# The first Q, K and V of an attention kernel, loaded whole or by thirds

## The chip, the cores and the metric

The kernel runs on one core of a Trainium2 chip. A core has engines that run side by side, each with its own stream of instructions: TensorE (PE in the profile, with its weight loads as PEld), VectorE (DVE), ScalarE (ACT), GpSimd (POOL) and SyncE (SP). In this kernel SP issues every transfer between the chip's memory and the core's on-chip memory. 16 DMA engines carry them. PE writes its results into PSUM, here eight banks of 128 x 512 words; the others work on SBUF and PSUM. An engine that needs another's result waits on a semaphore.

The metric is the device time of one execution, in microseconds (us). Three runs of the kernel before gave 119.02, 119.18 and 119.19 us; the median is 119.18.

## The reference

A linear attention with cosine weights is followed by a mixture of low-rank adapters. Everything is float32; the inputs are eight batches of eight heads with 576 positions of 64 numbers.

```python
theta = np.pi / 2.0 * pos / S
def phi(x, c, s):
    r = np.maximum(x, 0.0)
    return np.concatenate([r * c, r * s], axis=-1)
q_p = phi(q, cos_w, sin_w)
k_p = phi(k, cos_w, sin_w)
kv = np.einsum('bhsf,bhsd->bhfd', k_p, v)   # per head: 128 x 64
z = np.sum(k_p, axis=2)
num = np.einsum('bhsf,bhfd->bhsd', q_p, kv)
den = np.einsum('bhsf,bhf->bhs', q_p, z)[..., None] + 1e-06
x = (num / den), heads side by side         # 4608 rows of 512
logits = x @ w_gate                         # 8 experts; the two largest count
w = softmax over the two
out = x + sum over the two: w_e * (x @ A[e]) @ B[e]
```

In the second half A[e] is 512 x 16 and B[e] is 16 x 512.

## The kernel before, in words

A batch's Q, K or V is one transfer of 1152 KB (batches 4 and 5, and 6 and 7, share one for Q and for K). In SBUF a position p of 0 to 63 holds nine neighbouring rows j = 0 to 8 of 64 numbers, for four heads, with the other four heads in partitions 64 to 127; so each partition gets four runs of 9 x 64 floats, 2304 bytes each, from memory.

The work is cut into named steps, and the text `ORDER` lists them in the order in which they are issued. Behind "=" stands the engine (S is ACT, V is DVE, G is POOL), behind "@" the buffer. Each engine does its own steps in the listed order; semaphores follow from the buffers. A program planned the text beforehand, with costs and times of its own, and the text is fixed in the file. The steps:

- `LQ0`, `LK0`, `LV0`, `LK1` ...: the loads, on SP (L388); `ldw` the three weight transfers (L356, L359, L361).
- `cK0.0` to `cK0.2` and `cQ0.0` to `cQ0.2`: cast a third of a batch (three of the nine j) to 16 bits, with the maximum with zero for K (L440, L442; Q at L302, L304, L306). `phiK0.j` and `phiQ0.j`: multiply the cast rows j by the tangent, which gives the second half of phi (L310, L313). `vs0.j`: V's row j times the cosine (L310, L313).
- `kv0.0` to `kv0.2`: 24 matmuls each for k_p^T v over three j, on PE (L500); they need the phiK and vs of these three j. `ke0` copies the result out of PSUM (L302, L306).
- `tq`: transposes Q for a tile of 128 rows on PE (L604); `eq` copies it out with the maximum with zero (L621, L623); `nd` multiplies it by kv (L647 with L662 where both halves are of one batch, L654 with L668 where they are of two); `rd` and `nx` divide (L687, L692); `tx` and `ex` transpose the result (L713, L302, L306); `za` multiplies by gate and A (L738); `mx`, `nt`, `ge`, `d`, `sg`, `w`, `zg` choose and weigh the experts (L749 to L783); `tz` and `ez` transpose that (L799); `dx` adds x and B's part (L837); `eo` copies out of PSUM (L302, L306); `st` stores three tiles or fewer (L855).
- `fill=n` puts n matmuls of no use on PE (L864), the first 41 of them while nothing has arrived.

A step of one load needs the whole transfer: `add_phi` gives every cast `[ld]` as what it waits for, and `vs` gives the loads of V. SP's transfers take turns on eight semaphores, so an issue also waits until the transfer eight issues before it has landed, where it has not been waited for already. There are 36 tiles; tiles 0 to 2 belong to batch 0, 3 to 5 to batch 1, 6 to 8 to both, and so on in pairs.

Of the kernel before, what the change touches and what calls it, by code (L numbers as in the profile page):

```python
# [86 lines left out]
phiQ3.0=S tx8@7 phiQ3.3=G tx9 eq10=S@1 zg5 phiQ3.4=G tq12@4 ex8=V@1 tz2@0 phiQ3.1=G za6@6 tz5@1
vs3.0=G@0 ez2=V@2 za7 za8 mx6@1 tq13 ez5=V@0 phiK3.1=G vs3.1=S phiQ3.5=V dx3@0 vs3.2=G
phiQ2.8=S eq12=V@0 dx4 vs3.4=G phiK3.0=S dx5@7 phiK3.2=G eo3=S@0 mx7 nd10@2 mx8 cQ3.2=G@2 eo5=V
nd11 phiQ3.2=S kv3.0@0 fill=2@7 rd10@0 vs3.3=G LQ6@0 nx10@3 vs3.7=S vs3.5=G phiQ3.8=S nt8=G  # L90
vs3.8=S phiK3.6=G ge8 tq14@2 phiK3.8=V phiK3.7=S phiQ3.6=G d8 tx10@4 phiQ3.7=V sg8 kv3.1
vs3.6=V cK4.0=S@0 w8=G tx11 cK4.1=V@4 LV6@0 za9@7 kv3.2 tq15 ex10=V@1 phiK4.3=G cK4.2=S@2 mx9@0
# [807 lines left out]
```

## Time and profile before

| | |
|---|---|
| median of three runs | 119.18 us |
| the profiled execution | 118.97 us |
| its span, first to last instruction | 117.2 us |
| mean granted TensorE clock | 0.985 of full |
| read and written | 28.85 MB and 9.44 MB |
| transfers on SP's queue | 15808 packets, 38.29 MB |

The profile is one execution. "Busy" is the time in which an engine worked; PE's is partly modelled, since matmuls overlap. A row of the timeline or of a group gives the line in the code, the engine, the operation, what it writes and reads with their shapes, and in brackets how long the engine stood idle before, with what ended the idle time. A row of the chain of waits is a stretch (start, duration) of the path that ended last, followed back from the end. Times in it count from the first instruction.

### The profile page before, as it was taken

The numbers are of one execution on the slowest core, as the hardware profiler recorded it, in microseconds if no ns is written. First come the engines' busy times: TensorE is split into PE (matmuls) and PEld (weight loads), VectorE is DVE, ScalarE is ACT, GpSimd is POOL, SyncE is SP. The second block draws the span as 40 slices with busy tenths as digits, with TensorE's granted clock in tenths as the row PEclk, the third lists the DMA queues.
The fourth block names the chain that finished last, engine by engine and source line by source line (L and its number), as shares of the span: only waits on it lengthen the run. The fifth ranks groups of instructions, "written<-read, shape, count | busy, mean of one in ns | idle before, by whom it ended". The sixth has DMA issues, their size and how long they took to land.

```text
span 117.2 us, 4510 instructions
## 1 busy us (share of the span) xinstructions
PE 97.0 (83%) x1930; PEld 72.4 (62%) x1939; DVE 86.0 (73%) x206; ACT 86.1 (73%) x132; POOL 62.2 (53%) x118
## 2 busy tenths in 40 slices
...
GB/s 42 401 399 391 390 392 392 392 304 395 392 389 391 391 391 391 385 393 389 388 393 385 392 385 391 388 417 424 363 56 6 233 299 19 168 369 163 336 394 187
DMA packets 15827, 38.57 MB, mean 329 GB/s; under 512 B 1728, under 2 KB 1728, under 8 KB 15808
## 3 DMA queue, kind: packets, MB, share of 16 engines
q1 hardware_dynamic: 15808, 38.29, 87.1%
...
q14 instruction: 4, 0.03, 0.1%
HBM read 28.85 MB, written 9.44 MB: 327 GB/s over the span
## 4 chain that ended last, share of the span: by engine, by line
PE 32%; DMA 27%; DVE 21%; issue 6%; POOL 6%; ACT 2%; SPq 2%; DVEq 0%; POOLq 0%
DMA v<-in_v_dram 27%; PE psum L837 8%; PE psum L604 7%; PE psum L738 5%; DVE qt L623 5%; PE psum L713 4%; DVE x L692 4%; PE psum L654 3%; POOL vb L313 2%; POOL qp L304 2%; SPq L388 2%; DVE xt L306 2%; DVE kp L313 1%; DVE rd L687 1%; POOL qp L313 1%
## 5 line engine op out<-in xcount | busy, mean ns | idle before, releaser
L604 PE MATMUL psum<-ident,qp 128*128 128x128 bf16 x288 | 21.4, 226 | 4.1 <-DVE qp L313 1.3
L692 DVE TENSOR_TENSOR x<-psum,rd 128x1024 bf16<-128x1024 f32 (+1 forms) x19 | 22.2, 1168 | 0.6
L604 PEld LDWEIGHTS <-qp 128*128 128x128 bf16 x288 | 18.0, 101 | 6.1 <-issue 2.3
L313 POOL TENSOR_SCALAR kp<-kp,tanw 128x256 bf16<-128x256 bf16 (+1 forms) x28 | 16.2, 590 | 5.7 <-ACT kp L440 3.1
L313 POOL TENSOR_SCALAR qp<-qp,tanw 128x256 bf16<-128x256 bf16 (+1 forms) x31 | 17.2, 569 | 3.7 <-ACT qp L302 3.4
L313 POOL TENSOR_SCALAR vb<-v,cosw 128x256 bf16<-128x256 f32 (+1 forms) x25 | 14.8, 604 | 7.7 <-DMA v<-in_v_dram 7.6
L440 ACT ACTIVATE kp<-k 128x768 bf16<-128x768 f32 (+1 forms) x12 | 12.4, 1055 | 5.8 <-DMA k<-in_k_dram 5.4
L623 DVE TENSOR_SCALAR qt<-psum 128x2048 bf16<-128x2048 bf16 x12 | 14.6, 1214 | 0.9 <-PE psum L604 0.8
L713 PE MATMUL psum<-ident,x 128*128 128x128 bf16 x144 | 12.1, 221 | 3.3 <-DVE x L692 3.2
L500 PE MATMUL psum<-vb,kp 64*128 64x65 bf16 x576 | 12.8, 190 | 2.2 <-issue 1.1
L304 POOL CAST qp<-q 128x768 bf16<-128x768 f32 (+1 forms) x9 | 9.8, 1107 | 9.0 <-DMA q<-in_q_dram 7.4
L864 PE MATMUL psum<-ident 128*128 128x512 bf16 (+1 forms) x53 | 13.3, 405 | 1.4 <-POOL ident masks.py:199 1.4
L837 PE MATMUL psum<-x,ident 128*64 128x512 bf16 (+1 forms) x47 | 13.4, 384 | 0.6 <-ACT zt L302 0.3
L738 PE MATMUL psum<-AW,xt 128*128 128x136 bf16 x144 | 13.0, 223 | 0.7 <-DVE m L749 0.5
L500 PEld LDWEIGHTS <-kp 64*128 64x128 bf16 x576 | 10.2, 94 | 4.4 <-issue 2.4
L713 PEld LDWEIGHTS <-x 128*128 128x128 bf16 x144 | 9.3, 114 | 4.6 <-DVE x L692 4.3
L621 ACT ACTIVATE qt<-psum 128x2048 bf16<-128x2048 bf16 (+1 forms) x7 | 11.3, 1628 | 0.4 <-PE psum L604 0.4
L654 PE MATMUL psum<-kv,qt 128*64 128x65 bf16 x384 | 9.8, 197 | 2.1 <-issue 1.2
L837 PE MATMUL psum<-Bb,zt 128*64 128x512 bf16 (+1 forms) x42 | 11.4, 379 | 0.1
L302 ACT COPY o<-psum 128x1024 f32<-128x1024 f32 (+1 forms) x11 | 8.7, 821 | 3.7 <-PE psum L837 3.5
L738 PEld LDWEIGHTS <-xt 128*128 128x128 bf16 x144 | 9.4, 98 | 3.2 <-issue 1.4
L302 ACT CAST qp<-q 128x768 bf16<-128x768 f32 (+1 forms) x8 | 7.9, 987 | 4.7 <-DMA q<-in_q_dram 4.7
...
## 6 DMA issues: line engine op xcount, KB each, us to landing
v<-in_v_dram SPq DMA_DIRECT2D x8, 1152.0 KB, 16.0
q<-in_q_dram SPq DMA_DIRECT2D x4, 1152.0 KB, 15.0
...
k<-in_k_dram SPq DMA_DIRECT2D x2, 2304.0 KB, 20.0
...
```

Source lines behind the costliest of these rows:

```text
L302: nc.scalar.copy(o_ap, i_ap)
L313: eng.tensor_scalar(out=o_ap, in0=i_ap, scalar1=by, scalar2=0.0, op0=ALU.mult, op1=ALU.add)
L440: nc.scalar.activation(o_ap, i_ap, AF.Relu)
L500: nc.tensor.matmul(out=psum[:, s + hp, h2 * W:(h2 + 1) * W], lhsT=kp[hp * 64:hp * 64 + 64, bi * H2 + h2, :], rhs=vb_t[hp * 64:hp * 64 + 64 ...
L604: nc.tensor.transpose(out=o_ap[:, h2, :, hi, :], in_=qv[:, bi * H2 + h2, :], identity=ident)
L623: nc.vector.tensor_scalar(out=o_ap, in0=i_ap, scalar1=0.0, scalar2=None, op0=ALU.max)
L654: nc.tensor.matmul(out=psum[hi * 64:hi * 64 + 64, s + g, x * W:(x + 1) * W], lhsT=qt[:, qi, h2, hp, hi, :], rhs=kv_t[KV[b]["kv"].slot][:, ...
L692: nc.vector.tensor_tensor(out=x_t[Y["x"].slot][:, 0:n].rearrange("p n (g i d) -> p (n g) i d", g=2, i=4), in0=f()[:, :, :, 0:D], in1=r().t ...
L713: nc.tensor.transpose(out=bank16(s, 1024)[:, i * 512 + c * 128:i * 512 + (c + 1) * 128], in_=xv[:, c, :], identity=ident)
L738: nc.tensor.matmul(out=psum[:, s, i * ZW:(i + 1) * ZW], lhsT=xt_t[Z["xt"].slot][:, zi, c, :], rhs=AW[:, c, :], start=(c == 0 and i == 0), ...
L837: nc.tensor.matmul(out=o, lhsT=w, rhs=r, start=not last, stop=bool(last), skip_group_check=True)
L864: nc.tensor.matmul(out=psum[:, s % 8, c:], lhsT=ident, rhs=warm[:, c:], start=s < 8, stop=True, skip_group_check=True)
```

## The change

The loads of batch 0 are cut in three along j: `LQ0`, `LK0` and `LV0` become nine transfers, `LQ0.0` to `LV0.2`, of 384 KB, each with runs of 3 x 64 floats, 768 bytes. A cast of batch 0 waits for its own third alone, and a `vs0.j` for the third that holds j. All other loads stay whole and in the same order. The text `ORDER` is another one throughout: it was planned anew, so steps change places and engines all through the kernel. Its six `fill` steps have 47, 4, 6, 3, 8 and 2 matmuls; the four of before have 41, 8, 4 and 2.

```diff
-    def load(dst, src, bs):
+    def load(dst, src, bs, c):
         ap = src[bs[0]:bs[0] + len(bs)].rearrange(
             "b (g hp) (p j) d -> (hp p) (b g) (j d)", hp=2, j=NJ)
+        if c is not None:
+            dst, ap = (a[:, :, 3 * D * c:3 * D * (c + 1)] for a in (dst, ap))
         nc.sync.dma_start(out=dst, in_=ap)
...
+        for c in range(3) if b == 0 else (None,):
+            def e_ld(e, G=G, nm=nm, bs=bs, nb=nb, c=c):
...
+            parts.append(add("L" + l + (f".{c}" if c is not None else ""), {"SP": 0.55}, [], e_ld,
...
+        lds[l] = (G, parts)
...
-            oc = add(f"c{nm}{b}.{c}", engs, [ld], e_cast, free=gone, ss=[o_ident])
+            oc = add(f"c{nm}{b}.{c}", engs, [parts[c % len(parts)]], e_cast, free=gone, ss=[o_ident])
...
-                          [lv for _, lv in Vs] + [o_vone], e_vs,
+                          [ps_[j // 3 % len(ps_)] for _, ps_ in Vs] + [o_vone], e_vs,
```

The first lines of `ORDER`, up to nd8, the last of the nine tiles of batches 0 and 1:

```diff
-half@3 ident fill=41@0 LQ0@3 LK0@0 LV0@0 pos tab LK1@1 LV1@1 LQ1@2 sig tan LQ2@1 ldw@2
-cQ0.0=S@0 cQ0.1=G@1 cQ0.2=G@2 LK2@2 phiQ0.5=G phiQ0.7=G LV2@2 cK0.2=S@1 cK0.1=V@2 cK0.0=V@3
-phiQ0.2=S phiK0.7=G phiK0.8=V phiK0.0=S phiK0.4=G phiK0.5=V phiQ0.1=S phiQ0.3=V phiQ0.4=S vone
-phiK0.2=S LK3@3 vs0.0=V@0 vs0.1=G phiQ0.0=S vs0.7=V phiQ0.6=G vs0.6=V vs0.5=S tq0@4 vs0.3=G
-phiK0.1=V phiK0.6=S tq1 vs0.2=G vs0.8=V phiK0.3=S kv0.0@6 vs0.4=V eq0=V@0 kv0.1 LQ3@0 cK1.0=S@4
-kv0.2 tq2@2 ke0=S@2 cK1.2=V@0 cK1.1=S@5 phiK1.0=V nd0@4 phiK1.6=V nd1 fill=8@0 phiK1.7=V
-phiK1.2=S rd0@0 phiQ0.8=V LV3@0 vs1.0=V@1 vs1.3=S vs1.4=G nx0@6 phiK1.1=S vs1.8=G vs1.2=S
-vs1.6=G phiK1.5=S vs1.5=V tx0@6 vs1.1=G phiK1.8=V phiK1.4=S phiK1.3=G kv1.0@0 vs1.7=S kv1.1
-LK4@0 cQ1.1=S@3 cQ1.0=V@4 kv1.2 tx1 phiQ1.0=V ke1=S@0 phiQ1.3=V phiQ1.5=G ex0=V@1 tq3 phiQ1.1=S
-phiQ1.4=G cQ1.2=S@0 eq2=V@1 phiQ1.2=G tq4@0 tq5 phiQ1.6=G LV4@1 cQ2.1=S@5 phiQ1.7=V nd2@2
-cQ2.2=G@3 nd3 tq6@6 eq4=S@0 rd2@2 tq7 phiQ1.8=G nx2@0 phiQ2.3=G awa=G eq6=V@1 cQ2.0=S@1 nd4@2
-nd5 za0@0 phiQ2.0=S phiQ2.1=G rd4@0 tq8@6 nx4@1 phiQ2.5=G tq9 phiQ2.7=G tx2@1 cK2.1=S@3 tx3
-phiQ2.2=G mx0@0 tx4@2 ex2=V@0 tx5 cK2.0=S@2 phiQ2.4=G za1 ex4=V@1 za3@1 phiK2.5=G za2 cK2.2=S@1
-mx1 phiK2.1=G za4 mx2 za5 mx3@1 mx4 phiK2.0=S nd6@2 phiK2.4=G mx5 ge2 nd7 fill=4@10 vs2.0=S@2
-vs2.1=G nt5=V rd6@2 vs2.2=S vs2.7=G nx6@4 vs2.4=S vs2.3=G phiK2.6=S phiK2.2=G vs2.5=V vs2.8=S
-tx6@4 vs2.6=G d5 tx7 phiK2.7=S kv2.0@2 phiK2.3=G LV5@2 ex6=V@0 cK3.1=S@4 phiK2.8=G kv2.1 LQ4@2
-eq8=V@1 phiQ2.6=G kv2.2 awb=S phiK3.3=G ke2=S@1 nt2=V phiK3.4=G nd8@4 d2 ge5 sg2 nd9 cK3.2=V@3
+half@3 ident fill=47@0 LQ0.0@3 LQ0.1 LQ0.2 pos LK0.0@0 tab LK0.1 LK0.2 LV0.0@0 LV0.1 sig tan
+LV0.2 cQ0.1=G@5 LK1@1 cQ0.0=V@0 LV1@1 cQ0.2=G@3 vone phiQ0.1=G LQ1@1 cK0.0=V@0 phiQ0.3=V
+phiQ0.2=V LQ2@0 cK0.1=V@3 phiK0.1=V ldw@2 cK0.2=S@2 phiK0.2=V phiQ0.6=V phiQ0.4=S phiK0.7=G
+phiK0.0=S vs0.0=G@0 LK2@2 phiK0.3=G vs0.5=V LV2@2 phiK0.8=G phiQ0.8=V phiK0.5=G phiQ0.5=V LK3@3
+vs0.7=S vs0.2=G vs0.3=V phiK0.6=S vs0.4=G vs0.1=V phiK0.4=S vs0.8=G vs0.6=S phiQ0.0=V kv0.0@2
+kv0.1 tq0@0 LQ3@2 cK1.2=S@1 cK1.0=V@4 tq1 kv0.2 cK1.1=S@5 phiK1.8=V tq2@4 fill=4@6 phiK1.0=V
+phiK1.7=V phiK1.2=S eq0=V@0 phiK1.5=G ke0=S@0 phiK1.4=G LV3@0 vs1.0=G@1 vs1.1=S nd0@0 nd1
+fill=6@6 vs1.8=S phiK1.6=G rd0@0 phiK1.1=S vs1.7=G vs1.3=V vs1.5=S vs1.4=G nx0@2 phiK1.3=S
+vs1.2=G vs1.6=S LK4@0 tx0@0 cQ1.0=S@1 cQ1.1=V@4 tx1 kv1.0@6 phiQ1.4=V phiQ1.3=G cQ1.2=S@2 kv1.1
+phiQ1.0=V phiQ1.1=G ex0=V@0 tq3 phiQ0.7=S phiQ1.2=G kv1.2 phiQ1.6=V phiQ1.5=S eq2=V@1 tq4@2
+ke1=S@2 LV4@1 tq5 cQ2.2=G@0 phiQ1.7=S tq6@0 eq4=V@0 cQ2.0=S@1 nd2@4 cQ2.1=G@5 nd3 tq7 fill=3@12
+awa=G rd2@1 phiQ2.4=S nx2@0 eq6=S@1 phiQ2.0=G phiQ2.6=V phiQ2.7=G nd4@2 phiQ1.8=V nd5 phiQ2.3=G
+tx2@6 phiQ2.5=S rd4@2 tq8@0 nx4@4 za0@7 cK2.2=S@0 za1 tx3 tq9 phiQ2.2=S phiK2.7=G mx0@1 nd6@2
+ex2=V@1 cK2.0=S@4 phiK2.6=G nd7 mx1 za3@6 phiK2.8=G rd6@0 cK2.1=S@3 za2 fill=8@10 phiQ2.1=V
+phiK2.1=G mx3@0 mx2 phiK2.0=V phiK2.4=S nt2=G vs2.0=V@2 vs2.4=G vs2.3=S ge2 d2 vs2.7=G nx6@1
+vs2.1=S vs2.8=G vs2.6=S vs2.5=G vs2.2=S phiK2.3=V tx4@2 tx6@3 phiK2.2=G eq8=V@1 sg2 LV5@2 tx5
+tx7 phiK2.5=G cK3.2=S@1 kv2.0@4 LQ4@0 w2=G kv2.1 ex4=V@0 awb=G ex6=S@1 kv2.2 cK3.1=V@5
+phiK3.7=G za4 za5 ke2=S@1 mx4 nd8@0 mx5 ge5 cK3.0=S@0 nt5=G nd9 zg2 phiK3.4=G tq10@4 rd8@2
...
```

Around kv6 and at the end:

```diff
...
-nd23 phiK6.7=V tq26@0 rd22@1 nx22@4 vs6.0=S@0,1 vs6.1=G za18@6 tx20@7 tx21 vs6.6=S tq27 vs6.2=G
-vs6.4=V tx22@2 tz17@3 vs6.3=S vs6.5=G tx23 ex20=V@1 za19 kv6.0@4 ez17=S@0 vs6.8=G ex22=V@0
-kv6.1 cQ6.2=S@2 za21@7 vs6.7=G eq26=V@1 dx15@2 cQ6.1=G@4 dx16 za20 mx18@1 eo15=S@5 za22 mx21@2
-za23 mx19 mx20 kv6.2 ge20 mx22 nt20=G phiQ6.2=V phiQ6.5=G nd24@0 ke6=S@1 d20 mx23 nd25 nt23=V
-sg20 kv7.0@4 d23 rd24@0 sg23 w20=G phiQ6.4=S nx24@2 phiQ6.7=G kv7.1 phiQ6.1=G kv7.2 ge23 w23=V
...
-eo29=S mx35@0 dx30@0 d34 nt35=G ge34 sg34 dx31 st29.0 d35 ge35 w34=G sg35 dx32@2 zg34 eo30=S@3
-w35=G zg35 eo32=V tz35@7 tz34@4 ez35=S@0 ez34=V@2 st32.0 dx35@7 dx33@0 eo35=S@0 dx34 st35.0
-eo33=S@2 st34.0
+cQ6.0=G@4 zg17 nd20@0 eo12=S@4 nd21 tz17@6 rd20@0 za18@7 nx20@0 ez17=S@1 tq24@4 phiQ6.2=G
+phiK6.2=S dx14@6 cQ6.1=G@0 phiQ4.7=S nd22@0 eo14=V nd23 mx18@0 tx20@6 st14.0 rd22@0 phiQ6.0=G
+tx21 phiQ6.3=S nx22@4 za19 st11.0 tq25 phiQ6.1=G ex20=S@1 mx19 dx15@2 vs6.0=S@0,1 vs6.8=V
+vs6.4=G dx16 tq26@0 eq24=V@1 eo15=S@5 tq27 vs6.5=G dx17@6 eq26=V@0 vs6.7=G nd24@2 eo17=S nd25
+vs6.6=G phiK6.1=S za20 st17.0 rd24@0 tx22@6 mx20 tq28@0 vs6.2=G vs6.1=S nx24@3 st5.0 tq29
+nt20=G vs6.3=S tx23 st2.0 cQ6.2=G@2 d20 kv6.0@2 ge20 sg20 ex22=V@0 phiQ6.4=S kv7.0@4 w20=V
...
+mx33@0 tz32@4 mx34 dx29@3 ez32=V@2 nt34=G tx35@5 d34 dx30@0 eo29=V ex35=S@0 dx31 ge34 sg34
+st29.0 za35@4 eo30=S@4 w34=G dx32@6 mx35@1 zg34 nt35=V tz34@7 eo32=S ge35 ez34=V@2 d35 dx33@2
+st32.0 sg35 dx34 w35=G zg35 eo33=S@2 tz35@0 ez35=V@0 dx35@6 st34.0 eo35=S@0 st35.0
```

More of the change, by code (lines that the diff above doesn't have):

```diff
@@ L87 @@
[L87 to L92, printed above, removed]
```

79 lines of the change are left out of this document (42 added, 37 removed).

## The prediction

> **What bounds the kernel now.** I read the busy shares first, then the busy time by stage, then the chain of waits, then the front of the timeline, and last the transfers.
>
> ```profile
> span 117.2 us, 4510 instructions
> PE 97.0 (83%) x1930; PEld 72.4 (62%) x1939; DVE 86.0 (73%) x206; ACT 86.1 (73%) x132; POOL 62.2 (53%) x118
> ```
>
> No engine is full on average, so the stages have to be looked at. Columns after the time: busy us of PE, weight loads, DVE, ACT, POOL, then PE clock, DMA share and GB/s.
>
> ```profile
> 25.00:28.00 3.00, 3.00 (x40) 3.00 (x41) 1.57 (x4) 2.39 (x2) 2.38 (x5) 0.50 1.02 366
> 40.00:60.00 20.00, 17.32 (x363) 13.32 (x363) 18.71 (x41) 17.16 (x25) 14.87 (x28) 1.00 1.05 389
> 60.00:80.00 20.00, 17.79 (x413) 14.73 (x412) 16.77 (x36) 16.23 (x19) 13.97 (x18) 1.00 1.05 395
> 80.00:112.00 32.00, 29.58 (x625) 22.51 (x628) 26.34 (x71) 24.13 (x39) 10.48 (x21) 1.00 0.54 218
> ```
>
> Until 80 us the transfers run without a gap at some 390 GB/s; from 80 us on PE is busy 29.58 of 32 us. From 40 to 60 DVE is fullest (18.71 of 20). At 25 to 28 the granted clock was 0.50. The chain says how these join:
>
> ```profile
> 3.15 15.07 DMA v<-in_v_dram
> 18.31 2.04 POOL vb L313 x4
> ...
> 63.08 16.57 DMA v<-in_v_dram
> ...
> 81.53 0.64 PE psum L500 x24
> ...
> 112.33 1.01 ACT o L302
> ```
>
> Two loads are on it: V1, which lands at 18.2, and V7, the last one, which lands at 79.7 and releases kv6. Between them, and behind V7, it is compute. So the change can act in three places: when the early data arrives, how PE, DVE and ACT are packed behind it, and how much PE work stands behind V7.
>
> The early arrivals, and the steps that answer to them:
>
> ```profile
> 1.36 10.57 PE L864 MATMUL psum<-ident 128*128 128x512 bf16 x41 [1.36 <-POOL ident masks.py:199]
> 1.77 0.50 SPq L388 DMA_DIRECT2D v<-in_v_dram  x1
> 6.20 0.83 ACT L302 CAST qp<-q 128x768 bf16<-128x768 f32 x1 [2.25 <-DMA q<-in_q_dram]
> 9.21 1.03 DVE L442 TENSOR_SCALAR kp<-k 128x768 bf16<-128x768 f32 x2 [5.87 <-DMA k<-in_k_dram]
> 12.22 1.34 DVE L313 TENSOR_SCALAR vb<-v,cosw 128x256 bf16<-128x256 f32 x3 [0.73 <-DMA v<-in_v_dram]
> 13.50 0.30 PE L500 MATMUL psum<-vb,kp 64*128 64x65 bf16 x8
> 15.24 0.84 ACT L440 ACTIVATE kp<-k 128x768 bf16<-128x768 f32 x1 [1.61 <-DMA k<-in_k_dram]
> 16.62 0.40 PE L647 MATMUL psum<-kv,qt 128*128 128x65 bf16 x8 [0.49 <-ACT kv L302]
> 22.48 0.83 ACT L302 CAST qp<-q 128x768 bf16<-128x768 f32 x1 [1.72 <-DMA q<-in_q_dram]
> 24.27 1.71 PE L604 MATMUL psum<-ident,qp 128*128 128x128 bf16 x16 [0.18 <-ACT qp L310]
> 25.61 0.83 ACT L302 CAST qp<-q 128x768 bf16<-128x768 f32 x1 [0.68 <-DMA q<-in_q_dram]
> 30.63 2.31 ACT L440 ACTIVATE kp<-k 128x768 bf16<-128x768 f32 x3 [1.15 <-DMA k<-in_k_dram]
> 33.64 1.31 ACT L310 ACTIVATE vb<-v,cosw 128x256 bf16<-128x256 f32 x3 [0.30 <-DMA v<-in_v_dram]
> 39.03 0.44 PE L654 MATMUL psum<-kv,qt 128*64 128x65 bf16 x16 [0.71 <-DVE qt L623]
> ```
>
> Q0, K0, V0, K1 land at 6.2, 9.2, 12.2, 15.2: 3.0 us for each 1152 KB. Q1 lands at 22.5, Q2 25.6, K2 30.6, V2 33.6; each time an engine had been waiting for it. 13.50 is kv0.0, 16.62 nd0, 39.03 nd8.
>
> **The transfers.** Nine transfers of 384 KB replace three of 1152 KB. The bytes stay; each row of 2304 bytes becomes three of 768, so 1536 packets become 4608: 3072 more, 192 more for each of the 16 DMA engines. The trace has one place with short runs, the expert weights (A: 1024 packets of 256 bytes). First the packets of 23.5 to 25 us and of 40 to 60 us, then A's and the gate's issue (start, duration) and their KB and time to landing:
>
> ```profile
> DMA packets 1185, 0.42 MB, mean 278 GB/s; under 512 B 1118, under 2 KB 1118, under 8 KB 1184
> ...
> DMA packets 3433, 7.79 MB, mean 389 GB/s; under 512 B 76, under 2 KB 76, under 8 KB 3428
> ```
> ```profile
> 11.49 2.88 SPq L356 DMA_DIRECT2D o<-in_moe_A_dram  x1
> 14.41 3.78 SPq L359 DMA_DIRECT2D o<-in_moe_w_gate_dram  x1
> ```
> ```profile
> o<-in_moe_A_dram SPq DMA_DIRECT2D x1, 256.0 KB, 15.0
> ...
> o<-in_moe_w_gate_dram SPq DMA_DIRECT2D x1, 16.0 KB, 12.3
> ```
>
> Two prices follow. By the rate: 0.42 MB took 1.5 us where 389 GB/s needs 1.08; 0.42 us over some 1000 packets more than long rows would have made, 63 for each DMA engine, is 6.7 ns each. By the landing: Q2 lands at 25.6, A at 11.49 + 15.0 = 26.5; 0.9 us for 256 KB that long rows bring in 0.67; 0.23 us over 57 packets is 4.0 ns. Times 192: 1.3 or 0.8 us. I take 1.0, between the two; a run of 768 bytes is nearer to the 256 of A than to anything free. Bounds: 0 (the long rows hide it), and 2.4: 1.3 plus a price for each of the six added transfers, at most 0.18 us, since the gate's 16 KB landed at 14.41 + 12.3 = 26.7, 0.2 after A.
>
> The Trainium skill, "DMA: Bandwidth & Descriptors", section "Why small descriptors are slow (HBM only)", gives a packet about three cycles beside its 32-byte beats: 27 for 768 bytes against 75 for 2304, so 81/75 or 8% more, by my estimate 0.24 us for each of the three tensors and 0.7 in all. With that the sum below would end 0.3 us lower.
>
> So the thirds land 1.12 us apart: Q0's at 4.3, 5.4, 6.5; K0's at 7.6, 8.7, 9.9; V0's at 11.0, 12.1, 13.2. The first third of a tensor comes 1.2 to 1.9 us earlier than the tensor did, the last third of V0 comes 1.0 us later, and so does every load behind it: K1 16.2, V1 19.2, Q1 23.5, K2 31.6, V2 34.6, V7 80.7. SP issues nine times at about 0.5 us, ahead of 1.12 us of transfer each. From the ninth issue on each also waits for the landing eight issues before (LV0.2 for LQ0.0 at 4.3, LK1 for LQ0.1 at 5.4). Five thirds or more are then still queued, 5 us of cover, so I cost this at nothing. The other loads, the weights and the stores keep their places on SP's queue, and POOL issues no transfer. If the cover were gone, each such issue would add its own gap; the w_gate step gives 0.2 us for one.
>
> **The order up to nd8.** Durations:
>
> ```profile
> L440 ACT ACTIVATE kp<-k 128x768 bf16<-128x768 f32 x8 | 6.5, 839 | 5.4 <-DMA k<-in_k_dram 5.4
> L310 ACT ACTIVATE vb<-v,cosw 128x256 bf16<-128x256 f32 x11 | 5.3, 500 | 0.8 <-DMA v<-in_v_dram 0.8
> L313 POOL TENSOR_SCALAR vb<-v,cosw 128x256 bf16<-128x256 f32 x16 | 8.0, 513 | 5.4 <-DMA v<-in_v_dram 5.3
> L313 DVE TENSOR_SCALAR vb<-v,cosw 128x256 bf16<-128x256 f32 x9 | 3.5, 416 | 1.2 <-DMA v<-in_v_dram 1.2
> L623 DVE TENSOR_SCALAR qt<-psum 128x2048 bf16<-128x2048 bf16 x12 | 14.6, 1214 | 0.9 <-PE psum L604 0.8
> ```
>
> A phi step (same width, 16-bit input) is taken at the vs step's 0.5 us on ACT and POOL and at 0.3, somewhat under its 0.42, on DVE; a kv part at 0.54 on PE (below the 0.64 of the chain's first, which it shares with a start).
> The new order doesn't use V0's first third early: on DVE vs0.5 stands ahead of vs0.1 and waits for the second third (12.1), with four steps behind it, so kv0.0 starts near 14.0. On ACT vs0.7 waits for the last third (13.2), and phiK0.6 and phiK0.4 stand behind it: kv0.1 near 14.8, kv0.2 at 16.9 behind tq0 and tq1. Six more fills at 0.26 us end near 13.5, before any of it, and cost nothing; if kv0.0 were ready at 12.6 they would cost 0.9. Then eq0 stands on DVE behind cK1.0 and three phi of K1 (16.2 to 18.2) and takes 1.2: nd0 near 19.4, 2.8 us later than now. That is slack for now: tx0 and kv1 want V1 anyway (19.2, then five steps of POOL to vs1.2: 21.8).
> Q1 at 23.5: cQ1.1 and cQ1.0 start at once on DVE and ACT, tq3 at 24.8, tq5 from 26.4 to 26.9, against 25.98 (24.27 + 1.71). K2 at 31.6 and V2 at 34.6: POOL does four vs2 and two phi (phiK2.2, phiK2.5) to 37.6; kv2.1 to 38.1, kv2.2 to 38.7, za4 and za5 0.5, nd8 at 39.2. It is 39.03 now. Counting the two orders, PE has exactly the same steps ahead of nd8 in both, so this is a fair mark: **+0.2 us**. With the transfers at their bounds it would be 38.2 (-0.8) and 40.6 (+1.6).
>
> **From nd8 to the end.**
>
> ```profile
> 94.62 0.53 PE psum L604 x8
> ...
> 95.83 0.37 PE psum L654 x16
> ...
> 107.68 0.43 PE psum L837 x2
> ```
> ```profile
> 79.73 1.96 ACT L310 ACTIVATE vb<-v,cosw 128x512 bf16<-128x512 f32 x3 [1.35 <-DMA v<-in_v_dram]
> ```
>
> Between nd8 and kv6.0 the new order gives PE eight steps more: dx15 to dx17 (0.43 each), nd24, nd25 (two halves of 0.37), tq28, tq29 (0.53) and za20 (left out of the price): 1.3 + 1.5 + 1.1 = 3.9 us that no longer stand behind V7. So V7 can land 1.0 us later without emptying PE: the work behind it covers it. Without that cover it costs 1.0. ACT waited 1.35 us for V7, and that wait grows, but what ACT then does is early enough for kv6.0 at its new place. I take 0.3 of the 1.0 for what other loads (V3, Q4) pass on: **+0.3 us**, bounds 0 and 1.0. The stores at the end swap: tile 35's eo35 (one tile) is last instead of eo33 (1.01 us, two tiles), but waits for ez35 and dx35 of its own; I cost that at zero, bounds -0.4 and +0.6 from these durations.
>
> Sum: the profiled execution took 118.97 us (span 117.2 and 1.8 around it); +0.2 and +0.3 make 119.5. It lies 0.2 below the median of the runs, 119.18, so the forecast is **119.7 us**, its own range 119.1 to 120.4.
>
> **Rivals.**
> *The late loads stay late (slower).* If V3, Q4 and V7 meet engines that wait, as K2 and V2 do at 30.6 and 33.6 with 1.15 and 0.30 us, the whole 1.0 us reaches the end, with nd8's 0.2: 118.97 + 0.2 + 1.0 and the 0.2 to the median, 120.4. Decided by whether PE waits just ahead of kv6.0. For it: DVE at 18.71 of 20 us can't catch up. Against: the 3.9 us.
> *The runs cost nothing and the repacking wins (faster).* With no price for 768 bytes all loads land as now, nd8 comes 0.8 us earlier, and with fewer steps behind V7 the end keeps it: 118.97 - 0.8 + 0.2 = 118.4. For it: PE is the bound behind 80 us, and 3.9 us less of it stand there. Against: the 278 GB/s. It decides when V0's last third lands at 12.3 or before.
> *The change does nothing*: the waits for V1, Q1 and K2 stay, no load behind them lands later, and the new order gains and loses alike: 119.2. It shares the middle of the forecast.
> *The transfers come apart.* If each of the six added transfers paid a price of its own that isn't hidden, as the gate's 0.2 us is the nearest row for, V0 lands 1.1 us later again: 120.8.
> The Trainium skill, same page, section "Measured (HBM→SBUF, 128 partitions, SWDGE, issued from GpSimd)", has it that transfers want 1 MiB or more to reach three quarters of the peak, and 384 KB are under that; by that rule this rival would hold. Here 1152 KB land 3.0 us apart with others queued behind, and the gate's 16 KB take 0.2, so the trace speaks against a cost for each.
>
> **Chances.** Forecast 0.38, loads stay late 0.28, faster 0.27, nothing 0.03, transfers apart 0.04. 0.2% is about what a measurement of this kernel can tell from no change, 0.24 us, so "same" is 118.94 to 119.42. Of the forecast's 0.38, 0.24 lies above that, 0.08 within and 0.06 below. Faster 0.27 + 0.06 = 0.33; same 0.08 + 0.03 = 0.11; slower 0.28 + 0.04 + 0.24 = 0.56. Range 117.9 to 121.2: the fast case less 0.5 (the swap of the last stores, with its bound of 0.4, and the scatter), and the late loads with one more stretch of PE at half clock, as at 25 to 28 us: 16 transposes took 1.71 us there and 2 x 0.53 elsewhere, so 0.7.
>
> **What would show it.** Right: V0's last third is first used near 13.2, V1 near 19.2, V7 at 80.7; nd0 near 19.4 with nothing waiting for it, nd8 at 39.2; PE without a gap before kv6.0. Wrong: V0's end at 12.3 or 14.3, nd8 off by over 0.5 us, a second stage of clock 0.50 between 14 and 28 us, or a wait on V6, V7 just ahead of kv6.0.

## The result, and the profile after

The changed kernel takes 120.28 us (120.24, 120.28 and 120.88) against 119.18: ratio 1.0113, 95% interval 1.0074 to 1.0152, slower by 1.1%. The profiled execution took 120.24 us. The two first lines of its page:

```profile
span 118.1 us, 4560 instructions
PE 98.7 (84%) x1954; PEld 73.2 (62%) x1954; DVE 85.9 (73%) x211; ACT 83.7 (71%) x126; POOL 61.5 (52%) x119
```

The totals say little: DVE and POOL are as busy as before, ACT less, PE 1.7 us more. The timeline of the changed kernel tells where the loads are first used and what PE makes of it (start, busy time, engine, line, work, and in brackets the idle time ahead with what ended it):

```profile
4.38 0.56 DVE L306 CAST qp<-q 128x768 bf16<-128x768 f32 x1 [1.03 <-DMA q<-in_q_dram]
8.77 0.56 DVE L450 TENSOR_SCALAR kp<-k 128x768 bf16<-128x768 f32 x1 [3.51 <-DMA k<-in_k_dram]
9.97 0.56 DVE L450 TENSOR_SCALAR kp<-k 128x768 bf16<-128x768 f32 x1 [0.26 <-DMA k<-in_k_dram]
11.18 0.84 ACT L448 ACTIVATE kp<-k 128x768 bf16<-128x768 f32 x1 [7.23 <-DMA k<-in_k_dram]
13.61 0.50 DVE L313 TENSOR_SCALAR vb<-v,cosw 128x256 bf16<-128x256 f32 x1 [2.48 <-DMA v<-in_v_dram]
14.84 0.51 ACT L310 ACTIVATE vb<-v,cosw 128x256 bf16<-128x256 f32 x1 [2.02 <-DMA v<-in_v_dram]
20.55 0.42 PE L655 MATMUL psum<-kv,qt 128*128 128x65 bf16 x8 [1.04 <-DVE qt L631]
33.01 0.84 ACT L448 ACTIVATE kp<-k 128x768 bf16<-128x768 f32 x1 [1.54 <-DMA k<-in_k_dram]
37.74 1.86 PE L721 MATMUL psum<-ident,x 128*128 128x128 bf16 x16 [2.42 <-DVE x L700]
39.53 1.94 PE L508 MATMUL psum<-vb,kp 64*128 64x65 bf16 x72
41.98 0.44 PE L662 MATMUL psum<-kv,qt 128*64 128x65 bf16 x16
81.33 0.49 DVE L313 TENSOR_SCALAR vb<-v,cosw 128x512 bf16<-128x512 f32 x1 [0.26 <-DMA v<-in_v_dram]
```

K0's thirds come 1.20 us apart (8.77, 9.97, 11.18) and V0's last two 1.23 (13.61, 14.84); by the whole loads of before a third is 1.005. But Q0's first third is there at 4.38, and from it to K0's first are 4.39 us for three thirds, 0.8 more than three times 1.20. V0's end is used at 14.84, where before it was 12.22: 2.6 us later. K2 is used at 33.01 (30.63 before), V7 at 81.33 (79.75 before).

The stages show the same: the last column, GB/s, of the kernel before and then of the changed one (3.1, 2.5 and 3.5 us of the loading, then the stage of the half clock):

```profile
4.40:7.50 3.10, 3.10 (x16) 1.42 (x15) 0.00 (x0) 0.83 (x1) 1.20 (x2) 1.00 1.05 405
7.50:10.00 2.50, 2.50 (x13) 1.09 (x12) 0.79 (x2) 0.79 (x2) 1.31 (x3) 1.00 1.06 394
10.00:13.50 3.50, 2.93 (x26) 1.58 (x25) 2.77 (x9) 3.50 (x10) 2.30 (x5) 1.00 1.05 392
```
```profile
4.40:7.50 3.10, 3.10 (x10) 1.13 (x9) 0.85 (x2) 0.00 (x0) 1.06 (x2) 1.00 1.06 327
7.50:10.00 2.50, 2.50 (x14) 1.11 (x12) 0.98 (x4) 0.00 (x0) 1.05 (x2) 1.00 1.10 337
10.00:13.50 3.50, 3.50 (x18) 1.58 (x17) 1.12 (x4) 1.64 (x3) 1.39 (x4) 1.00 1.10 333
37.60:41.10 3.50, 3.36 (x75) 3.16 (x76) 2.57 (x5) 2.12 (x4) 2.99 (x7) 0.51 1.06 393
```

From 7.5 us on it is some 335 GB/s instead of 393, while the DMA engines are fully taken up (share 1.10). The chain of waits of the changed kernel goes through V2, then through a PE that had waited 2.42 us and starts again at half clock, from there through PE, DVE and ACT alone to kv6 at 85.85, and at the very end through tile 35 alone. No load behind V2 is on it, not even V7:

```profile
24.06 11.93 DMA v<-in_v_dram
...
36.55 1.14 DVE x L700
...
37.74 1.86 PE psum L721 x16
...
79.76 1.24 DVE x L700
...
82.99 1.19 DVE qt L631
...
84.67 1.13 DVE x L700
...
85.85 0.91 PE psum L508 x48
...
112.44 0.30 DVE zg L791
...
113.76 0.59 ACT o L302
```

Before, the last copy was 1.01 us long and held two tiles; here it is 0.59 and one. So three things stand side by side: loads 2.6 us later, an nd8 that is 2.95 us later (41.98 against 39.03), and a span only 0.9 us longer. Something gives 2 us back.

### The profile page after: what moved, and what is told of

Read it like the earlier page. It is cut to its first block, busy times and chain, and to the rows that moved or that the text cites. A ratio compares the mean times of both kernels' runs of the same rounds, so it can differ in the third digit from the quotient of the medians.

```text
span 118.1 us, 4560 instructions
## 1 busy us (share of the span) xinstructions
PE 98.7 (84%) x1954; PEld 73.2 (62%) x1954; DVE 85.9 (73%) x211; ACT 83.7 (71%) x126; POOL 61.5 (52%) x119
## 4 chain that ended last, share of the span: by engine, by line
PE 37%; SPq 19%; DVE 16%; DMA 10%; ACT 8%; issue 6%; POOL 0%; POOLq 0%; DVEq 0%; ACTq 0%
SPq L390 11%; DMA v<-in_v_dram 10%; PE psum L845 10%; DVE x L700 7%; PE psum L612 7%; PE psum L721 6%; SPq L359 5%; PE psum L746 5%; PE psum L508 4%; PE psum L662 4%; ACT qt L629 3%; SPq L356 3%; PE psum L807 2%; DVE qt L631 1%; DVE m L757 1%
## 5 line engine op out<-in xcount | busy, mean ns | idle before, releaser
L313 POOL TENSOR_SCALAR kp<-kp,tanw 128x256 bf16<-128x256 bf16 (+1 forms) x29 | 16.4, 577 | 15.7 <-ACT kp L448 15.6
L612 PE MATMUL psum<-ident,qp 128*128 128x128 bf16 x288 | 20.4, 219 | 1.1 <-DVE qp L313 0.7
L872 PE MATMUL psum<-ident 128*128 128x512 bf16 (+1 forms) x70 | 17.5, 405 | 1.4 <-POOL ident masks.py:199 1.4
L313 POOL TENSOR_SCALAR vb<-v,cosw 128x256 bf16<-128x256 f32 (+1 forms) x30 | 17.4, 595 | 1.6 <-DMA v<-in_v_dram 1.4
L721 PE MATMUL psum<-ident,x 128*128 128x128 bf16 x144 | 13.3, 230 | 4.4 <-DVE x L700 4.2
L721 PEld LDWEIGHTS <-x 128*128 128x128 bf16 x144 | 10.5, 117 | 7.5 <-issue 3.4
L302 ACT COPY o<-psum 128x1024 f32<-128x1024 f32 (+1 forms) x12 | 9.9, 840 | 6.6 <-PE psum L845 6.5
L845 PE MATMUL psum<-Bb,zt 128*64 128x512 bf16 (+1 forms) x48 | 13.7, 379 | 0.3 <-DVE zt L306 0.2
L872 PEld LDWEIGHTS <-ident 128*128 128x128 bf16 x70 | 7.2, 107 | 9.6 <-issue 3.6
L313 POOL TENSOR_SCALAR qp<-qp,tanw 128x256 bf16<-128x256 bf16 (+1 forms) x20 | 11.5, 583 | 1.7 <-DVE qp L306 1.4
L788 POOL TENSOR_TENSOR w<-ge,ex 128x24 f32<-128x24 f32 (+2 forms) x10 | 2.3, 232 | 18.6 <-ACT ex L784 18.6
```

The costliest lines, as they stand in the source:

```text
L313: eng.tensor_scalar(out=o_ap, in0=i_ap, scalar1=by, scalar2=0.0, op0=ALU.mult, op1=ALU.add)
L612: nc.tensor.transpose(out=o_ap[:, h2, :, hi, :], in_=qv[:, bi * H2 + h2, :], identity=ident)
L721: nc.tensor.transpose(out=bank16(s, 1024)[:, i * 512 + c * 128:i * 512 + (c + 1) * 128], in_=xv[:, c, :], identity=ident)
L845: nc.tensor.matmul(out=o, lhsT=w, rhs=r, start=not last, stop=bool(last), skip_group_check=True)
L872: nc.tensor.matmul(out=psum[:, s % 8, c:], lhsT=ident, rhs=warm[:, c:], start=s < 8, stop=True, skip_group_check=True)
```

## The experiments

Theory after the first look: the order is worth a gain by itself, and the thirds cost more than it brings. Rival: the order is worth nothing, and the lateness is hidden in part. All ratios are to the kernel before, run on the same chip.

| kernel | median us (lowest to highest) | ratio, 95% interval |
|---|---|---|
| new order, whole loads | 117.92 (117.68 to 118.18) | 0.990, 0.9887 to 0.9913 |
| old order, thirds | 121.37 (120.51 to 121.92) | 1.0183, 1.0157 to 1.021 |
| old order, cut by heads | 119.98 (119.39 to 120.34) | 1.0064, 1.0042 to 1.0087 |
| changed kernel, tile 35 early | 121.68 (120.82 to 123.12) | 1.0205, 1.0162 to 1.0249 |
| new order, V0 alone by thirds | 118.26 (118.25 to 118.49) | 0.9927, 0.9909 to 0.9945 |
| new order, cut by heads | 118.53 (117.77 to 119.01) | 0.9942, 0.9916 to 0.9968 |
| new order, Q0 alone by thirds | 118.53 (118.0 to 119.33) | 0.9959, 0.9932 to 0.9987 |
| new order, whole loads, tile 35 early | 119.45 (119.32 to 119.58) | 1.0025, 1.0016 to 1.0035 |
| new order, whole loads, tile 35's last steps ahead of 34's | 119.2 (118.92 to 119.23) | 0.9999, 0.9989 to 1.0009 |
| changed kernel again, twice | 120.69 (119.59 to 121.21), 120.02 (119.54 to 120.94) | 1.0113, 1.0059 to 1.0167; 1.0077, 1.0043 to 1.011 |
| changed kernel, three thirds under way | 123.06 (122.35 to 123.38) | 1.0315, 1.0275 to 1.0356 |

**The new order with whole loads.** Only the loads of batch 0 are undone:

```diff
-half@3 ident fill=47@0 LQ0.0@3 LQ0.1 LQ0.2 pos LK0.0@0 tab LK0.1 LK0.2 LV0.0@0 LV0.1 sig tan
-LV0.2 cQ0.1=G@5 ...
+half@3 ident fill=47@0 LQ0@3 pos LK0@0 tab LV0@0 sig tan
+cQ0.1=G@5 ...
-        for c in range(3) if b == 0 else (None,):
+        for c in (None,):
```

> The new order, with the first Q, K and V loaded whole as before (one part of the change undone, nothing left out of the computation). Theory L (the short runs delay every load by 2.4 us, and that is what is paid for): V0 lands near 12.2 us, V1 near 18.2 and V2 near 33.6 as before, nd8 starts at 39.6 us or earlier (41.98 with thirds), and the time is 119.2 us or less, ratio 0.99 to 1.00. Theory O (the new order itself is slower, through nd0 that comes late and the chain of tile 35 at the end; the loads are hidden): nd8 stays at 41 to 42 us and the time near 120.2, ratio 1.01.

117.92 us: 1.26 faster than before, 2.36 faster than the changed kernel. So the order is a gain, and the thirds cost 2.4 us of time where the forecast had 1.3 (its 119.7 against its own 118.4 for loads without a price). V7 is on its chain of waits (the first line); below it the timeline at V7 and at the end:

```profile
63.04 16.48 DMA v<-in_v_dram
```
```profile
79.61 0.49 DVE L313 TENSOR_SCALAR vb<-v,cosw 128x512 bf16<-128x512 f32 x1 [0.90 <-DMA v<-in_v_dram]
80.02 2.35 DVE L631 TENSOR_SCALAR qt<-psum 128x2048 bf16<-128x2048 bf16 x2
82.56 1.23 DVE L700 TENSOR_TENSOR x<-psum,rd 128x1024 bf16<-128x1024 f32 x1
83.84 0.91 PE L508 MATMUL psum<-vb,kp 64*128 64x65 bf16 x48
...
109.04 0.28 PE L807 MATMUL psum<-ident,zg 128*128 128x128 bf16 x2 [0.16 <-DVE zg L791]
110.68 1.64 ACT L302 COPY o<-psum 128x1024 f32<-128x1024 f32 x2 [0.58 <-PE psum L845]
110.76 0.23 PE L807 MATMUL psum<-ident,zg 128*128 128x128 bf16 x1 [0.16 <-DVE zg L791]
```

DVE waits for V7, and kv6 starts on PE 4.23 us after that step (83.84 against 79.61): the wait isn't on PE but on DVE, ahead of the two `qt` and the `x`. `ORDER` shows why: `vs6.8=V` stands ahead of `eq24=V`, which nd24 needs, and kv6.0 writes the PSUM buffer that nd24 wrote (both `@2`), so it starts only when `nx24`, that `x`, has read it. In the six kernels of the new order whose chain goes through V7 (here and in the runs below) the distance is 4.22 or 4.23 us each time, with V7 used anywhere from 79.61 to 81.66: there its lateness goes straight through to kv6.

In the changed kernel it is 4.52 (85.85 against 81.33), and 4.86 and 4.87 in its two repeats below. There V7 is not on the chain: earlier loads (V2 in the profile above, K loads in the repeats) come so late that the work behind them reaches kv6 0.3 to 0.6 us after V7 would have allowed. So two late paths lie nearly level: V7 alone would have put kv6 at 81.33 + 4.23 = 85.56. From kv6 on the lateness stays: 2.01 us against whole loads at kv6, 2.03 at the last copy (113.76 against 111.73).

**The old order with the thirds.**

```diff
-half@3 ident fill=41@0 LQ0@3 LK0@0 LV0@0 pos tab LK1@1
+half@3 ident fill=41@0 LQ0.0@3 LQ0.1 LQ0.2 LK0.0@0 LK0.1 LK0.2 LV0.0@0 LV0.1 LV0.2 pos tab LK1@1
```

> The old order, with nine transfers of runs of 768 bytes in the places of the three and each step waiting for its own third (the other part of the change alone). Theory L: V0's last third is used near 14.6 us, V1 lands near 20.6, V2 near 35.9; the old order leaned on early loads, so nd8 moves from 39.0 to about 41 us and the time to 120.3 to 121.6, ratio 1.010 to 1.020. Theory O: the loads land as late, but the time stays within 0.3 us of before, ratio 1.000 to 1.003.

121.37: the thirds cost 2.19 us in the old order too (2.36 in the new one). With a scatter of 1.4 us in this kernel's runs, no difference between the orders is shown.

**The old order, nine transfers with long runs.** Each tensor is cut by heads (2, 1 and 1 of the four a partition has), so every run is 2304 bytes; all steps wait for all three parts.

```diff
-            dst, ap = (a[:, :, 3 * D * c:3 * D * (c + 1)] for a in (dst, ap))
+            dst, ap = (a[:, (0, 2, 3)[c]:(2, 3, 4)[c]] for a in (dst, ap))
```

> The old order, with nine transfers in place of three, but cut by heads (two heads, one, one), so that the runs keep their 2304 bytes; each step waits for all three. It tells the length of the runs from the number of transfers. If the run length is the price: V0 is whole at 12.2 to 12.5 us, V1 at 18.2 to 18.6, and the time is within 0.3 us of before, ratio 1.000 to 1.003. If each transfer has a price: V0 is whole near 13.5 to 14.6 and the time 0.5 to 1.5 us up.

119.98: 0.8 us slower than before without any short run, and 1.4 faster than the thirds. So the cutting costs something by itself. What the length of the runs costs is not quite told by the 1.4, since here all steps wait for the whole tensor and with the thirds they don't.

**The changed kernel with tile 35 early.** The last output hangs on tile 35's chain alone, so its steps are moved ahead (`tx35`, `ex35`, `za35`, `mx35`, and the choice of its experts beside tile 34's):

```diff
-... nt34=G tx35@5 d34 dx30@0 eo29=V ex35=S@0 dx31 ge34 sg34
-st29.0 za35@4 eo30=S@4 w34=G dx32@6 mx35@1 zg34 nt35=V tz34@7 eo32=S ge35 ez34=V@2 d35 ...
+... tx35@5 ... ex35=S@0 ... nt34=G za35@4 d34 mx35@1 dx30@0 nt35=V eo29=V dx31 ge34
+ge35 d35 sg34 sg35 st29.0 eo30=S@4 w34=G w35=G dx32@6 zg34 zg35 tz34@7 tz35@5 ...
```

> The changed kernel, with the steps of the last tile, 35, moved ahead of the last big outputs, as the old order has them (only the last three lines of the order are changed). If the single chain at the end (tile 35 through max, weights, transpose, output) costs what its waits show, PE has no idle stretch of over 0.3 us behind 110 us and the time falls by 0.3 to 0.7 us against 120.3, ratio to before 1.005 to 1.009. If the end is bound by PE's work alone, it stays at 120.3, ratio 1.011.

121.68: 1.4 slower, not faster. Its loads come as late as in the changed kernel (V0's end at 14.90 us) and its runs lie 2.3 us apart, so it is repeated below with whole loads.

**Which part of the cutting costs.** Three kernels in the new order: V0 alone by thirds; all three by heads; Q0 alone by thirds.

```diff
-        for c in range(3) if b == 0 else (None,):
+        for c in range(3) if l == "V0" else (None,):
```

> The new order, with Q0 and K0 whole and only V0 by thirds (five transfers instead of nine to the end of V0). Theory: a third with 768-byte runs takes 0.2 us more than a third of a whole transfer (1.20 us against 1.005 in the two traces), and a second loss, single DMA engines that stand still for about 1 us between 4.4 and 7.5 us, comes only with many transfers issued early. Then V0's last third lands at 12.2 + 0.6 = 12.8 us, no engine falls behind, and the time is 117.9 + 0.6 = 118.5 us or a little less, since the first third of V0 can be used earlier. Rival (any cut load brings the standstill): V0 at 13.8, time 119.3. Rival (the loads' lateness is hidden in the new order): 117.9.

> The new order, nine transfers cut by heads (2, 1 and 1 of four) so that every run is 2304 bytes long; the steps wait for all three parts. Theory (two losses, run length 1.8 us and standing engines about 1 us): only the second is left, V0 lands at 13.2 to 14.3 us, time 117.9 + 0.8 to 1.5 = 118.7 to 119.4 us. Rival (run length is all of it): V0 at 12.2 and 117.9 us. Rival (the number of transfers is all of it): 120.3 us, as the nine thirds.

> The new order, with K0 and V0 whole and only Q0 by thirds (five transfers to the end of V0, as in the run with V0 alone by thirds, but the short ones come first). Theory (single engines stand still when the first transfers of the program are cut, whatever the count): packets of 0.3 us and more between 4.4 and 7.5 us, Q0's last third over 7 us, V0 at 12.14 + 0.6 + 0.5 to 2 = 13.2 to 14.7, time 118.5 to 120. Rival (it takes many transfers issued at once): no packet over 0.25 us, V0 at 12.7, K1 at 15.7, time 117.9 + 0.4 to 0.6 = 118.4.

V0 alone: +0.34 us on the whole loads. V0's last third landed at 12.78, 0.64 later than whole, as 3 x 0.2 says. By heads: +0.61. Q0 alone: +0.61, but its runs lie between 118.0 and 119.33, and the profiled one is the slowest of them. The stages of 4.4 to 7.5 us and of 10 to 13.5 us, of V0 alone, of heads, and of Q0 alone; and last the first of the two for heads in the old order:

```profile
4.40:7.50 3.10, 3.10 (x13) 1.21 (x12) 1.33 (x2) 0.00 (x0) 1.23 (x2) 1.00 1.04 404
10.00:13.50 3.50, 3.50 (x18) 1.56 (x16) 3.23 (x10) 1.49 (x5) 3.35 (x6) 1.00 1.08 349
```
```profile
4.40:7.50 3.10, 3.10 (x11) 1.21 (x10) 0.29 (x1) 0.00 (x0) 0.27 (x1) 1.00 0.94 277
10.00:13.50 3.50, 3.50 (x18) 1.57 (x17) 2.36 (x8) 1.80 (x4) 1.11 (x2) 1.00 1.04 404
```
```profile
4.40:7.50 3.10, 3.10 (x16) 1.36 (x14) 0.81 (x2) 0.00 (x0) 0.82 (x1) 1.00 1.05 351
10.00:13.50 3.50, 3.13 (x15) 1.28 (x14) 2.15 (x7) 1.64 (x3) 0.94 (x1) 1.00 1.06 392
```
```profile
4.40:7.50 3.10, 3.10 (x14) 1.28 (x13) 0.00 (x0) 0.00 (x0) 0.00 (x0) 1.00 0.93 285
```

That parts two losses. Short runs cost while they run: 349 GB/s in V0's thirds. With long runs cut by heads the rate is 404 once it is going, so the number of transfers costs nothing there; but between 4.4 and 7.5 us it is 277. In the trace single packets then take up to 0.95 us, where 0.09 is usual. The trace has 16 marks for the landing of each load, as many as there are DMA engines, and from then on one to five of them come over 0.4 us behind the middle one. A load is used only after its last mark, so everything behind is late: in the changed kernel half of the marks of V0's last third were there at 13.50 and the last one at 14.76 (first use 14.84), with V0 alone by thirds 12.57 and 12.78.

This came at the start of every kernel whose first load, Q0, is cut (eight profiled executions, lags of 0.9 to 2.3 us in Q0's last part; the ninth, with few loads issued, is told below), and in none where Q0 is whole (the kernel before and four of the new order: lags of 0.1 to 0.2 us, no packet over 0.21 us between 3 and 9 us). Five transfers are enough for it if Q0 is among the cut ones, and the same five don't bring it if V0 is; so it isn't the number. Nor is it the early work on the first thirds: with heads in the old order DVE, ACT and POOL do nothing from 4.4 to 7.5 us, and the rate is 285 all the same.

**How many lie issued.** Two kernels were to hold SP back, so that four, or two, loads are under way:

```diff
+    seq = [o for l in "Q0 K0 V0 K1 V1 Q1".split() for o in lds[l][1]]
+    for o, d in zip(seq[4:], seq):
+        o.deps = [d]
```

> The changed kernel with one thing added: from the fifth load on to Q1, each is issued only when the load four before it has landed, so that at most four are under way. Theory (standing engines come from the number of transfers that lie issued): no packet over 0.3 us between 4.4 and 7.5 us, spacing of the thirds stays 1.20 us, V0's last third at about 13.5 us instead of 14.8 and the time 120.3 - 1.2 = 119.1 us. Rival (they come from the cutting, however few are issued): V0 at 14.5 or later, 120.3 us. If the waits starve the queue, the DMA share between 3 and 14 us falls below 0.95 and the time is over 120.3.

> The changed kernel with each load from the third on (to Q1) issued only when the load two before it has landed, so that never more than two are under way. The run with four under way did not hold SP back: its issues came within 0.4 us of the changed kernel's. Theory (engines stand because of what is issued early): no packet over 0.3 us between 4.4 and 9 us; but from issue to landing takes 3.6 us at the least, so two thirds in 3.6 us instead of 1.2 each: a third every 1.8 us, V0 at about 18 us and the time 123. Rival (they stand for what the cut first transfers themselves are): long packets again, with no more than two transfers under way. The verdict is in the packets, not in the time.

Neither did: such an entry is only looked at when the written order is read, and a wait comes from buffers that overlap. Both are the changed kernel again, and what they tell is its scatter: 119.54 to 121.21, with the middle between 120.0 and 120.7, and V0's end landed at 15.16 and 15.02 (14.76 in the first profile). Kernels with whole loads stay within 0.5 us. The third try has the waits, from a copy of one column on ACT:

```diff
-LQ0.2 pos LK0.0@0 tab LK0.1 LK0.2 LV0.0@0 LV0.1 sig tan
+LQ0.2 pos tab sig tan LK0.0@0 LK0.1 LK0.2 LV0.0@0 LV0.1
...
+            seen.append(dst)
+            if len(seen) > 3:
+                nc.scalar.copy(dst[:, 0, 0:1], seen[-4][:, 0, 0:1])
         nc.sync.dma_start(out=dst, in_=ap)
```

> The changed kernel, and this time waits that are there: ahead of each of K0's and V0's thirds stands a copy of one column on ScalarE, from the third three places before it into the place that this one fills, so that SP issues it only when that third has landed; at most three thirds are under way, and the position tables go ahead of the copies on ScalarE. (The two runs with four and two under way had no such waits: an order named among the loads alone makes none, and they are the changed kernel run again.) From issue to landing takes 3.6 us at the least, 2.4 of it before a third's first bytes, and two thirds still under way are 2.4 us of transfer, so the queue just keeps up or starves by 0.3 to 0.5 us every third. Theory (the standing engines come from what lies issued in the first 5 us): no packet over 0.3 us from 4.2 to 9 us and each third's 16 engines finish within 0.6 us of each other, V0's last third at 13.5 to 15.0 us. Rival (they come with cut transfers at the program's start, however few are issued): a packet of 0.5 us or more between 4.2 and 7.5 us, one engine 0.8 to 2 us behind the others from then on, V0 at 14.8 to 16.5. By the time the two differ less: 119.6 to 120.5 against 120.3 to 121.5 us.

Its stages, and the copy on ACT that waits for Q0's last third:

```profile
4.40:7.50 3.10, 3.10 (x11) 1.22 (x10) 0.83 (x2) 0.52 (x3) 1.62 (x2) 1.00 1.01 284
10.00:13.50 3.50, 3.50 (x18) 1.57 (x17) 1.15 (x4) 1.92 (x5) 0.82 (x2) 1.00 0.88 250
```
```profile
6.67 0.19 ACT L394 COPY k<-q 128x1 f32<-128x1 f32 x1 [0.95 <-DMA q<-in_q_dram]
```

Issued three at a time, Q0's thirds come 1.2 us apart to the end: the last is used at 6.67, where in the other kernels with Q0 by thirds it landed at 7.2 to 8.7. But then packets of 0.6 to 0.85 us come all the same, at 7.2 to 8.4 and 11.9 to 15.4 us, and V0's end is at 16.2. So the theory falls as it stood: few under way is no cure. Of the rival the packets came (the first just inside its 4.2 to 7.5 us, most later) and V0's end did, but not the time: 123.06 is beyond both forecasts. A DMA share of 0.88 says that the queue also starved here, so this run adds a loss of its own and is no clean test of the count. (The 2.4 us that the expectation puts ahead of a third's first bytes are too many for the first one: it is issued at 0.74 us and its first packet starts at 1.85.) Why engines stand still stays open.

**The tail, with whole loads.** Once with tile 35's steps early as above, once with only its last steps ahead of tile 34's, as in the kernel before:

```diff
-... nt35=V tz34@7 eo32=S ge35 ez34=V@2 d35 dx33@2
-st32.0 sg35 dx34 w35=G zg35 eo33=S@2 tz35@0 ez35=V@0 dx35@6 st34.0 eo35=S@0 st35.0
+... nt35=V eo32=S ge35 d35
+st32.0 sg35 w35=G zg35 tz35@0 tz34@7 ez35=S@0 ez34=V@2 dx35@6 dx33@2 eo35=S@0 dx34 st35.0 eo33=S@2 st34.0
```

> The new order with whole loads, and the last steps reordered as in the run with tile 35's steps ahead of the last outputs. If that run's loss (121.7 against 120.3) came with its loads, the tail itself is worth its shorter chain, 117.9 - 0.3 = 117.6 us (117.3 to 117.9). If it came from the tail, 117.9 + 0.5 to 1.4 = 118.4 to 119.3 us.

> The new order with whole loads, but the last outputs in the order of the kernel before: tile 35's last steps ahead of tile 34's. The prediction put the swap at 0 (-0.4 to +0.6): 117.9 us, 117.3 to 118.3. Rival (from the run with tile 35's steps early, which lost 1.5 us against the same loads): tile 34's results are ready 1.7 us before tile 35's, TensorE waits for tile 35 with tile 34 queued behind it, 117.9 + 0.7 to 1.5 = 118.6 to 119.4 us.

119.45 and 119.2: in the new order the swap of the last outputs is worth 1.28 us, and with it taken back the new order as a whole is worth nothing (ratio 0.9999). The end of the timeline with the swap taken back:

```profile
108.81 0.41 DVE L791 TENSOR_TENSOR zg<-psum,w 128x256 bf16<-128x256 f32 x1
110.37 0.29 DVE L791 TENSOR_TENSOR zg<-psum,w 128x128 bf16<-128x128 f32 x1 [0.88 <-POOL w L788]
110.72 0.34 PE L807 MATMUL psum<-ident,zg 128*128 128x128 bf16 x3 [1.60 <-DVE zg L791]
112.64 1.01 ACT L302 COPY o<-psum 128x1024 f32<-128x1024 f32 x1 [0.32 <-PE psum L845]
```

Tile 34's `zg` is done at 109.22 (108.81 + 0.41), yet PE waits 1.60 us for tile 35's (110.37 + 0.29), with tile 34's transposes queued behind it; the last copy ends at 113.65. In the new order PE took tile 34's at 109.04, its output went while tile 35's was made, and the last copy ended at 112.32 (110.68 + 1.64). With tile 35's steps early, last of all, the loss comes on DVE:

```profile
108.31 0.17 DVE L757 MAX8 m<-psum 128x8 f32<-128x8 f32 x1 [0.94 <-PE psum L746]
109.19 0.24 DVE L779 TENSOR_TENSOR ge<-psum,m 128x16 f32<-128x16 f32 x2
110.24 0.46 PE L807 MATMUL psum<-ident,zg 128*128 128x128 bf16 x3 [0.68 <-DVE zg L791]
112.45 1.01 ACT L302 COPY o<-psum 128x1024 f32<-128x1024 f32 x1 [1.25 <-issue]
```

DVE waits 0.94 us for tile 35's gate values with tile 34's `ge` queued behind: both tiles are chosen together from 109.19 on, and both end late. It is the same loss in two places: a tile that is ready stands behind one that is not. Whether the swap would do the same in the old order was not run. The trace of the kernel before speaks against as much: there the `zg` of the two tiles are made back to back, and PE waits 0.24 us for them:

```profile
109.45 0.73 DVE L783 TENSOR_TENSOR zg<-psum,w 128x256 bf16<-128x256 f32 x2
110.23 0.34 PE L799 MATMUL psum<-ident,zg 128*128 128x128 bf16 x3 [0.24 <-DVE zg L783]
```

So it is the new order that has tile 34 ready early and tile 35 late (110.66 with the swap taken back, against 110.18), and the swap that turns this into a gain.

## Why the prediction was right, and where it was not

The forecast was 119.7 with its own range of 119.1 to 120.4; 120.28 lies in that, on the side that had the greater chance. That the sum came so near is in part luck, for two errors partly cancel. The thirds cost 2.36 us, where the forecast had 1.3 for them (119.7 against its 118.4 without their price). The order gave 1.26 (117.92 against 119.18), where the forecast had 0.8, and it gave them in another place: the 0.8 was nd8's and did not reach the end, the 1.28 is the tail's, which had been put at zero.

*"Times 192: 1.3 or 0.8 us. I take 1.0."* The term was too small. A third took 1.20 us instead of 1.12, so the nine cost 1.8 by the length of their runs, some 9 ns for each of the 192 added packets instead of 5; V0 alone by thirds (+0.64 at its landing) and the rate of 404 GB/s with long runs show that it is the length. The bound of 2.4 was needed, but for another reason than the six added transfers: 0.8 us come from the engines that stand still at the start (4.39 us for the first three thirds instead of 3.6), which no row of the kernel before shows. V0's end at 14.84 is past the 14.3 that was to prove the step wrong. The small-packet rule of the Trainium skill, "DMA: Bandwidth & Descriptors", section "Why small descriptors are slow (HBM only)", 8% here, was further off: the measured spacing gives 19%.

*"Five thirds or more are then still queued, 5 us of cover, so I cost this at nothing"*, and the rival of the transfers that come apart. Once going, nine transfers by heads run at 404 GB/s and cost nothing each, as the step said. The rule of 1 MiB or more of the Trainium skill, "DMA: Bandwidth & Descriptors", section "Measured (HBM→SBUF, 128 partitions, SWDGE, issued from GpSimd)", by which that rival would have held, doesn't show at these 404 GB/s. The standing engines at the start do fall on the rival's side: 0.61 us with long runs.

*The order up to nd8, +0.2.* As a time for nd8 its own part was right: with whole loads nd8 came at 38.07, where the working gave 38.2 for no price. But the sum added nd8's time to the end as it stood, and that failed: with whole loads and the old tail nd8 came at 38.16, 0.9 earlier than before, and the time is that of before (119.2). There the chain goes through V7, and V7 is used at 79.90 against 79.75.

In the profile of the changed kernel nd8 came at 41.98, beyond the upper bound of 40.6; in its two repeats at 41.23 and 39.75. Two things of the 41.98 were not in the sum. K2 was used 2.4 us later than before, 1.0 more than Q1 and Q2, which landed 1.4 later. And PE's wait of 2.42 us for `x` was followed by a stage at a clock of 0.51, in which 16 transposes took 1.86 us and 72 matmuls 1.94 (1.05 and 1.27 at that place with whole loads). The clock alone doesn't make the loss, nor does the length of the wait alone make the clock: in the repeat with 41.23 PE waited 2.89 us at that place, the transposes took 1.05 us again, and that execution took 120.62 us. A second such stage had been named as what would be wrong, for 14 to 28 us; here the one of before (25 to 28 us) is gone, the clock there is 1.00, and this one came at 37.6. nd0 at 20.55 (19.4 forecast) passed without harm of its own, as the step said: the chain doesn't go through it.

*"V7 can land 1.0 us later without emptying PE: the work behind it covers it."* This failed. It counted PE's steps, rightly, but the one who waits for V7 is DVE (L313), and behind that wait stand the two `qt` and the `x` that nd24 and kv6.0 need: a part of the cover itself stands behind V7. In the six new-order kernels with V7 on their chain kv6 starts 4.22 or 4.23 us after DVE's step on V7, however late V7 is. In the changed kernel the late loads reached kv6 by the other path, V2 and the work behind it, 0.3 us after V7's. So the rival "the late loads stay late" named the right mechanism, though its deciding point, PE waiting just ahead of kv6.0, is not what shows it: PE has work up to 85.80, and the wait is DVE's (0.26 us in the changed kernel, 0.90 with whole loads).

*"I cost that at zero, bounds -0.4 and +0.6."* The swap of the last outputs was worth -1.28. The step compared the lengths of the last copies (1.01 and 0.59); what counted was who is queued behind whom on PE: with the old tail in the new order tile 34 was ready 1.4 us before tile 35 and stood behind it.

*The rival "the runs cost nothing and the repacking wins", 118.4*: with the loads' price taken away the order gives 117.92. Its sign was right, its reason not: nd8's lead is lost on the way, and the gain shows only with the swapped tail.

The fastest kernel here is the new order with the loads left whole, 1.0% faster than before (117.92 us).
